# Attention and two feed-forward layers on one core: raw words' places in another order, small softmax operations on DVE, layer 1's weight casts on POOL

## The chip, the cores and the metric

The kernel runs on one core of a Trainium2 chip. A core has the engines PE (matrix products), DVE, ACT and POOL (element-wise work), SP (which issues the DMA transfers here) and DMA queues, all running beside each other and tied by semaphores. The metric is the device time of one execution in microseconds, smaller is better. PE has a clock that the chip grants: 2.4 GHz, or 1.2 GHz at the half level.

## The reference

Attention with 4 batches, 8 heads, 576 positions and 64 values per head; its output, as 2304 tokens of 512 values, goes through two feed-forward layers of width 2048. All inputs are float32.

```python
scores = scale * np.matmul(q, k.transpose(0, 1, 3, 2))
mask_local = (rel >= 0) & (rel < 32)                          # heads 0 to 3
mask_strided = (rel >= 0) & (pos[None, :] % 32 == pos[:, None] % 32)   # heads 4 to 7
scores = np.where(masks[None], scores, -1000000000.0)
attn = np.exp(scores - np.max(scores, axis=-1, keepdims=True))
attn = attn / (np.sum(attn, axis=-1, keepdims=True) + 1e-09)
x = np.matmul(attn, v)             # as (2304, 512)
...
h = np.maximum(x @ w_in, 0.0)      # layer 1
x = h * h @ w_out
...
h = x @ w_in                       # layer 2, weights of its own
P = a[0] + a[1] * h + a[2] * h * h + a[3] * h * h * h
Q = 1.0 + np.abs(b[0]) * np.abs(h) + np.abs(b[1]) * h * h
out = P / (Q + 1e-6) @ w_out
```

## The kernel before

**Precision.** Every operand of layer 1 and layer 2 is kept as a high part (PE's rounded float32 form, `fp32r`) and a low part, the rest. A product is three matmuls: high by high, high by low, low by high.

**Blocks and units.** The tokens are cut into 6 blocks of 384 columns (`j`), the width of 2048 into 16 tiles of 128 (`f`). `h_unit` (matmuls at L457) makes the hidden tile `f` of a block in 12 matmuls, into one PSUM bank `h`; ACT makes its relu `r` (L467) and square, then the high part `gh` (L474), and DVE or POOL the low part `gl` (L475). `o_unit1` (L497) adds the tile's share to four output banks `acc` in 12 matmuls, two steps later. Layer 2 does the same from 523 us of the profile on, with the rational function on DVE.

**Attention.** There are 48 groups of two heads and up to two tiles, 12 for a batch, taken in pairs (a and b). A group is: scores on PE (`ps_s`, L296); their maxima on DVE (L307); these scaled by -1/8 (L308, on POOL); exponentials on ACT with the scaled maximum as bias, which also sum up (L320); 1e-9 added to the sums (L328, on POOL); the reciprocal on DVE (L329); the scaling of the exponentials on POOL (L331); transposes on PE (`ps_t`, L338), a copy (L344, L346); the products with v on PE (`ps_v`, L354); the output's high part on ACT (L379) and low part on DVE (L380). L308, L328 and L329 work on the group's small tile `sm`, up to 4 columns each. The first 12 groups run ahead of layer 1 (`at_slot`), the others are dealt out as pieces between the units of layer 1 (`at_piece`).

**Weights of layer 1.** They lie in DRAM as 64-bit words and come during block 0 as 32 halves of 512 KB (in a name like `wraw_7_1`, 7 is the tile `f`; 0 is its share of w_in, which `h_unit` needs, 1 its share of w_out, for `o_unit1`). `wq` sets their order: 0_0, 1_0, 2_0, 0_1, 3_0, 1_1 and so on; 16 to 27 are 9_0, 7_1, 10_0, 8_1, 11_0, 9_1, 12_0, 10_1, 13_0, 11_1, 14_0, 12_1, and 15_0, 13_1, 14_1, 15_1 are last. `load_raw` (L189) issues the loads on SP in that order; the scheduler may reorder them. The list `homes` names the place in SBUF into which each half's raw words go: a tile that will later hold the high (`h12`) or low part (`l12`) of the weights of a tile `f`, free until then, or, with `None`, one of three stage buffers. A half may only be loaded when its place has been read by whoever had it before.

`to_f32` turns a half into float32: ACT L201 takes the absolute value, scaled; DVE L202, L203 and L204 put the bits together (the intermediate lies in a PSUM bank, `bits`, for layer 1, in SBUF for layer 2). `split_w` then makes the high part `wh` (on ACT at L218 for every fourth half, on POOL at L220 otherwise) and the low part `wl` by subtraction (L221, on POOL but for the first four). From block 1 on, layer 2's weights go through the same functions and out to DRAM.

**Order.** The tile framework's scheduler sets each engine's order from the program's order and its own costs. An engine runs its list strictly in order; an instruction that waits holds all behind it. There are 7 PSUM banks named `ps`; in block 0, `acc` holds four, and `ps_s`, `ps_t`, `ps_v` and `h` share three.

Of the kernel before, what the change touches and what calls it, by code (L numbers as in the profile page):

```python
# [14 lines left out]
ALU = mybir.AluOpType  # L15
# [11 lines left out]
NF = DFF // P  # L27
# [129 lines left out]
def moe_kernel(ctx, tc, qk, vp, w1, w2, a, b, masks, eye, out):  # L157
    nc = tc.nc
# [54 lines left out]
    def split_w(wh, wl, wf):  # L213

        halves[0] += 1
        n = halves[0]
        if n % 4 == 0:
            nc.scalar.copy(wh, wf)  # L218
        else:
            nc.gpsimd.tensor_scalar(wh, wf, 1.0, 0.0, ALU.mult, ALU.add)  # L220
        (nc.vector if n <= 4 else nc.gpsimd).tensor_tensor(wl, wf, wh.bitcast(F32), ALU.subtract)  # L221
# [79 lines left out]
    def at_max(n):  # L301
        g, s = groups[n], st[n]
        nn = s["nn"]
        if n >= LATE:
            nc.vector.tensor_tensor(s["to"], s["to"], s["mask"], ALU.add)
        sm = s["sm"] = apool.tile([P, 16], F32, tag="sm", name=f"sm{g.name}", bufs=6)
        nc.vector.tensor_reduce(sm[: g.nq, 0:nn], s["ps"], AX.X, ALU.max)  # L307
        nc.gpsimd.tensor_scalar(sm[: g.nq, 4 : 4 + nn], sm[: g.nq, 0:nn], -1.0 / 8.0, 0.0, ALU.mult, ALU.add)  # L308

    def at_exp(n):  # L310
        g, s = groups[n], st[n]
# [13 lines left out]
    def at_norm(n):  # L325
        g, s = groups[n], st[n]
        sm, nn = s["sm"], s["nn"]
        nc.gpsimd.tensor_scalar(sm[: g.nq, 8 : 8 + nn], sm[: g.nq, 8 : 8 + nn], 1.0, 1e-9, ALU.mult, ALU.add)  # L328
        nc.vector.reciprocal(sm[: g.nq, 12 : 12 + nn], sm[: g.nq, 8 : 8 + nn])  # L329
        r = sm[: g.nq, 12 : 12 + nn, None].to_broadcast([g.nq, nn, g.nk])  # L330
        nc.gpsimd.tensor_tensor(s["e"], s["e"], r, ALU.mult)  # L331
# [62 lines left out]
    def at_slot(n):  # L394

        load_groups(n + 4)
        if n % 2 == 0:
            at_scores(n)
        at_max(n)
        if n == 2:  # L400
            warm_up(2)
        for m in range(max(0, n - 4), n):
            if n - m == lags(m)[1]:
                at_values(m)
        for m in range(max(0, n - 4), n):
            if n - m == lags(m)[0]:
                at_transpose(m)
        at_exp(n)
        for m in range(max(0, n - 4), n):
            if n - m == lags(m)[1]:  # L410
                at_out(m)
        at_norm(n)
# [14 lines left out]
    def at_piece(piece):  # L427
        nonlocal slot
        if isinstance(piece, int):
            at_scores(piece)  # L430
            for n in (piece, piece + 1):
                at_max(n)
                at_exp(n)
                at_norm(n)
            load_qk(piece // 2 + 2)
            return
        v, t = piece
        if v < NG:
            at_values(v)
            slot = max(slot, v + 5)  # L440
        if t < NG:
            at_transpose(t)
        if v < NG:
            at_out(v)
            if v % 2 and v // 2 + 2 >= AHEAD_PAIRS:
                load_v(v // 2 + 2)
# [81 lines left out]
    def load_co():  # L528
# [9 lines left out]
    homes = [  # L538
        ("h8", 0), ("h9", 0), ("h15", 1), ("h14", 3), ("h13", 5), ("h12", 7), ("h11", 9), ("l11", 9), ("h10", 11), ("l10", 10), ("l9", 11), ("l8", 12),
        ("l15", 13), ("l14", 14), ("l13", 15), ("l12", 16),  # L540
    ]
    homes += [(c + str(f), 0) for f in (12, 13, 14, 15, 14, 15) for c in "hl"] + [(None, 0)] * 4
    raws = []

    def load_raw(done):
# [11 lines left out]
    def feed_w(n):  # L557
        for _ in range(n):
            load_raw(fed[0])
            if fed[0] < len(wq):  # L560
                f, part = wq[fed[0]]
                c = slice(part * DM, (part + 1) * DM)
                wh, wl = wt[0, f] if part else w_place(0, f)
                split_w(wh[:, c], wl[:, c], to_f32(0, f, part, raws[fed[0]]))
                fed[0] += 1
# [14 lines left out]
    def spill_w(f, part):  # L580

        wf = to_f32(1, f, part, load_w(1, f, part))
        parts = [stage.tile([P, DM], F32R, tag="w32", bufs=3, name=f"sp{c}{f}_{part}") for c in "hl"]
        split_w(*parts, wf)
        for z, t in enumerate(parts):
            nc.sync.dma_start(w2_dram[z, f][:, part * DM : (part + 1) * DM], t.bitcast(F32))
# [161 lines left out]
```

## Time and profile before

| what | value |
|---|---|
| median of 3 runs | 929.36 us (928.68 to 929.71) |
| the profiled execution | 929.01 us, of which 927.2 us from the first to the last instruction |
| busy: PE, DVE, POOL, ACT | 899.6, 674.2, 599.1, 548.1 us |
| chain of work that ended last, by engine | DVE 44%, PE 43%, POOL 4%, ACT 4%, DMA 3%, issue 2% |
| its lines | L624 24%, L457 20%, L497 17%, L626 9%, L635 7%, all others 2% or less |

The profile is one execution. The shares are means over stages with different limits, so the time is read by stage: the first 42 us load operands and do the first groups of the attention; from 42 us layer 1's block 0 runs while its weights are converted; from 146 us layer 1's blocks 1 to 5, with the rest of the attention and the conversion of layer 2's weights; from 523 us layer 2.

### The profile page before, as it was taken

The page shows a single profiled execution, that of the slowest core. Times are in us where ns is not written, and L with a number is a line of the kernel's source. Part 1 is how long each engine was busy: PE and PEld are TensorE (multiplying, and loading weights), DVE is VectorE, ACT ScalarE, POOL GpSimd, SP SyncE. Part 2 cuts the span into 40 slices and gives each one's busy share as a digit, 9 for nine tenths or more (in the row PEclk, how much of TensorE's full clock was granted, in tenths as well). Part 3 has the DMA queues.
Part 4 walks back from the last instruction along what each step waited for, and adds up shares of the span by engine and source line. Part 5 has one row for each costly group of instructions (what it writes and reads, how often), then busy time and mean ns, then how long its engine had stood idle before and what let it go on. Part 6 is the DMA issues. An engine that isn't in the chain of part 4 may idle for free.

```text
span 927.2 us, 14645 instructions
## 1 busy us (share of the span) xinstructions
PE 899.6 (97%) x5232; PEld 825.7 (89%) x5232; DVE 674.2 (73%) x792; ACT 548.1 (59%) x1392; POOL 599.1 (65%) x643
## 2 busy tenths in 40 slices
PE   7799889999999999999999999999999999999998
PEld 4698789998998899999999999899999899899896
DVE  3887774645554554635312689999999999999997
ACT  5785564445444444433324577676776777777774
POOL 3676664554554545544333488888888888888885
PEclk9799899999999999999999999999999999999999
DMA  7863235444444543442377620010010100100000
GB/s 282 316 231 121 92 109 177 160 144 155 131 147 140 174 121 122 162 138 78 123 254 253 218 70 9 18 43 10 23 37 10 51 19 1 43 1 1 35 1 34
DMA packets 40104, 98.55 MB, mean 106 GB/s; under 512 B 4704, under 2 KB 11616, under 8 KB 40032
## 3 DMA queue, kind: packets, MB, share of 16 engines
q1 hardware_dynamic: 40032, 97.62, 31.5%
q8 instruction: 41, 0.67, 0.3%
q14 instruction: 31, 0.25, 0.1%
HBM read 71.39 MB, written 26.21 MB: 105 GB/s over the span
## 4 chain that ended last, share of the span: by engine, by line
DVE 44%; PE 43%; POOL 4%; ACT 4%; DMA 3%; issue 2%; POOLq 0%; SPq 0%; DVEq 0%; ACTq 0%
DVE rq L624 24%; PE h L457 20%; PE acc L497 17%; DVE p L626 9%; DVE rq L635 7%; PE ps_s L296 2%; PE ps_v L354 2%; POOL wl L221 2%; PE ps_t L338 2%; ACT e L320 1%; DVE wraw L204 1%; DMA qk<-in_qk 1%; DMA wraw<-in_w 1%; DVE bits L203 1%; ACT w L201 1%
## 5 line engine op out<-in xcount | busy, mean ns | idle before, releaser
L457 PE MATMUL h<-xh,wh 128*128 128x384 f32 x768 | 264.8, 345 | 3.8 <-ACT r L467 2.3
L457 PE MATMUL h<-xh,wl 128*128 128x384 f32 x768 | 259.6, 338 | 0.0
L457 PE MATMUL h<-xl,wh 128*128 128x384 f32 x768 | 259.1, 337 | 0.0
L624 DVE RECIPROCAL rq<-w 128x384 f32<-128x384 f32 x96 | 243.9, 2541 | 17.3 <-POOL w L622 17.3
L457 PEld LDWEIGHTS h<-xh,wh 128*128 128x128 f32 x768 | 145.8, 190 | 12.0 <-issue 2.6
L457 PEld LDWEIGHTS h<-xl,wh 128*128 128x128 f32 x768 | 145.8, 190 | 3.8
L457 PEld LDWEIGHTS h<-xh,wl 128*128 128x128 f32 x768 | 145.4, 189 | 0.0
L643 POOL TENSOR_TENSOR gl<-rq,gh 128x384 fp32r<-128x384 f32 x96 | 114.7, 1195 | 40.1 <-ACT gh L642 40.1
L475 POOL TENSOR_TENSOR gl<-r,gh 128x384 fp32r<-128x384 f32 x75 | 76.1, 1015 | 88.4 <-ACT gh L474 73.1
L497 PE MATMUL acc<-gh,wl 128*128 128x384 f32 x384 | 129.5, 337 | 2.2 <-POOL wl L221 2.2
L497 PE MATMUL acc<-gh,wh 128*128 128x384 f32 x384 | 129.3, 337 | 1.3 <-ACT wh L218 0.9
L497 PE MATMUL acc<-gl,wh 128*128 128x384 f32 x384 | 128.5, 335 | 0.0
L622 POOL TENSOR_TENSOR w<-w,sq 128x384 f32<-128x384 f32 x96 | 97.8, 1019 | 46.7 <-ACT sq L619 46.7
L623 POOL TENSOR_TENSOR p<-p,hs 128x384 f32<-128x384 f32 x96 | 115.0, 1198 | 0.0
L657 PE MATMUL acc<-wh,gl 128*128 128x512 f32 x288 | 114.0, 396 | 0.3 <-POOL gl L643 0.3
L657 PE MATMUL acc<-wl,gh 128*128 128x512 f32 x288 | 113.7, 395 | 0.0
L657 PE MATMUL acc<-wh,gh 128*128 128x512 f32 x288 | 112.1, 389 | 0.5 <-ACT gh L642 0.5
L642 ACT CAST gh<-rq 128x384 fp32r<-128x384 f32 x96 | 49.4, 515 | 106.5 <-DVE rq L635 106.5
L471 DVE TENSOR_TENSOR r<-r 128x384 f32<-128x384 f32 x75 | 51.7, 689 | 81.9 <-ACT r L467 81.5
L626 DVE SCALAR_TENSOR_TENSOR p<-p,co,hs 128x384 f32<-128x384 f32 x96 | 100.0, 1042 | 0.0
L467 ACT ACTIVATE r<-h 128x384 f32<-128x384 f32 x91 | 44.9, 493 | 91.7 <-PE h L457 84.1
L474 ACT CAST gh<-r 128x384 fp32r<-128x384 f32 x91 | 46.9, 515 | 64.9 <-DVE r L471 64.4
(77 smaller groups left out, 1577.7 us busy)
## 6 DMA issues: line engine op xcount, KB each, us to landing
wraw<-in_w SPq DMA_DIRECT2D x64, 512.0 KB, 4.3
w_scratch<-sph SPq DMA_DIRECT2D x32, 256.0 KB, 4.1
w_scratch<-spl SPq DMA_DIRECT2D x32, 256.0 KB, 3.3
wh<-w_scratch SPq DMA_DIRECT2D x16, 512.0 KB, 3.6
wl<-w_scratch SPq DMA_DIRECT2D x16, 512.0 KB, 4.6
v<-in_vp SPq DMA_DIRECT2D x24, 256.0 KB, 4.2
qk<-in_qk SPq DMA_DIRECT2D x12, 416.0 KB, 4.1
x_scratch<-x SPq DMA_DIRECT2D x24, 192.0 KB, 2.5
```

What stands on the lines that cost most here:

```text
L457: nc.tensor.matmul(ps[:, :TB], w[:, c], x[:, kk, :], start=(kk == 0 and i == 0), stop=(kk == KT - 1 and i == 2))
L471: nc.vector.tensor_tensor(h, h, h, ALU.mult)
L475: low = lambda: (nc.vector if psum_h or j == 0 else nc.gpsimd).tensor_tensor(gl, h, gh.bitcast(F32), ALU.subtract)
L497: nc.tensor.matmul(acc[j][e][:, :TB], w[:, c], g, start=(f == 0 and i == 0), stop=(f == NF - 1 and i == 2))
L622: keep(nc.gpsimd.tensor_tensor(w, w, sq, ALU.add))
L623: keep(nc.gpsimd.tensor_tensor(p1, p1, hs, ALU.mult))
L624: keep(nc.vector.reciprocal(rq, w))
L626: keep(nc.vector.scalar_tensor_tensor(p1, p1, a1, hs, ALU.add, ALU.mult))
L635: keep(nc.vector.scalar_tensor_tensor(rq, p1, a0, rq, ALU.add, ALU.mult))
L642: keep(nc.scalar.copy(gh, rq))
L643: keep(nc.gpsimd.tensor_tensor(gl, rq, gh.bitcast(F32), ALU.subtract))
L657: nc.tensor.matmul(p, g[:, t * P : (t + 1) * P], w[:, c], start=(f == 0 and i == 0), stop=(f == NF - 1 and i == 2))
```

## The change

Three edits. (1) The halves 16 to 27 get places in another order, and three of them, with the number 23 to 25, stage buffers instead. (2) The scaling of the maxima (L308) and the addition to the sums (L328) are DVE's instead of POOL's, in all 48 groups. (3) Every fourth cast stays on ACT only for layer 2's weights; the 8 of layer 1's are POOL's. The arithmetic is the same.

```diff
-        if n % 4 == 0:
+        if n % 4 == 0 and n > 2 * NF:
             nc.scalar.copy(wh, wf)
         else:
             nc.gpsimd.tensor_scalar(wh, wf, 1.0, 0.0, ALU.mult, ALU.add)
...
-        nc.gpsimd.tensor_scalar(sm[: g.nq, 4 : 4 + nn], sm[: g.nq, 0:nn], -1.0 / 8.0, 0.0, ALU.mult, ALU.add)
+        nc.vector.tensor_scalar(sm[: g.nq, 4 : 4 + nn], sm[: g.nq, 0:nn], -1.0 / 8.0, 0.0, ALU.mult, ALU.add)
...
-        nc.gpsimd.tensor_scalar(sm[: g.nq, 8 : 8 + nn], sm[: g.nq, 8 : 8 + nn], 1.0, 1e-9, ALU.mult, ALU.add)
+        nc.vector.tensor_scalar(sm[: g.nq, 8 : 8 + nn], sm[: g.nq, 8 : 8 + nn], 1.0, 1e-9, ALU.mult, ALU.add)
...
-    homes += [(c + str(f), 0) for f in (12, 13, 14, 15, 14, 15) for c in "hl"] + [(None, 0)] * 4
+    homes += [(x, 0) for x in ("h12", "h13", "h14", "h15", "l15", "l14", "l13", None, None, None, "h15", "l15")] + [(None, 0)] * 4
```

Three places of the order that the scheduler makes of it. Names: `wraw_7_1` is a half's raw words, `sm_0_0` the small tile of the group with heads 0 and 1 (the first number) and part 0 (the second), `sm_1_0` its partner's. A number at the end tells buffers apart.

SP's list, the loads behind those of 9_0, in block 0. Before:

```order
L189 DMA wraw_12_0_962<-in_w 128x1024
L189 DMA wraw_15_0_1242<-in_w 128x1024
L264 DMA v_2_2_863<-in_vp 128x512
L189 DMA wraw_13_1_1244<-in_w 128x1024
L189 DMA wraw_14_1_1246<-in_w 128x1024
L529 DMA co<-in_a 128x4
L251 DMA qk_0_1_941<-in_qk 128x832
L530 DMA co<-in_b 128x2
L189 DMA wraw_10_1_964<-in_w 128x1024
L189 DMA wraw_9_1_960<-in_w 128x1024
L189 DMA wraw_8_1_956<-in_w 128x1024
L189 DMA wraw_7_1_952<-in_w 128x1024
```

After, from 9_0 on:

```order
L189 DMA wraw_9_0_724<-in_w 128x1024
L189 DMA wraw_7_1_734<-in_w 128x1024
L189 DMA wraw_10_0_800<-in_w 128x1024
L189 DMA wraw_8_1_810<-in_w 128x1024
L189 DMA wraw_10_1_964<-in_w 128x1024
L189 DMA wraw_13_0_1024<-in_w 128x1024
L264 DMA v_2_2_869<-in_vp 128x512
L189 DMA wraw_11_1_1034<-in_w 128x1024
```

7_1 stood last of the twelve rows, behind 10_1, 9_1 and 8_1; it now stands next to 9_0, and 8_1 and 10_1 follow before 13_0.

DVE's list at the first pair of batch 1 (the groups 0_0 and 1_0), between the halves 8_1, 11_0 and 9_1. Before:

```order
L307 TENSOR_REDUCE sm_0_0_1205<-ps_s_0_0_1193 96x4
L202 TENSOR_SCALAR bits_1_1075<-w_0_8_1_1074 128x512
L307 TENSOR_REDUCE sm_1_0_1216<-ps_s_1_0_1194 96x4
L203 SCALAR_TENSOR_TENSOR bits_1_1075<-wraw_8_1_956,bits_1_1075 128x512
L204 SCALAR_TENSOR_TENSOR wraw_8_1_956<-wraw_8_1_956,bits_1_1075 128x512
L329 RECIPROCAL sm_0_0_1205<-sm_0_0_1205 96x4
L202 TENSOR_SCALAR bits_0_1085<-w_0_11_0_1084 128x512
L203 SCALAR_TENSOR_TENSOR bits_0_1085<-wraw_11_0_958,bits_0_1085 128x512
L204 SCALAR_TENSOR_TENSOR wraw_11_0_958<-wraw_11_0_958,bits_0_1085 128x512
L329 RECIPROCAL sm_1_0_1216<-sm_1_0_1216 96x4
```

After:

```order
L307 TENSOR_REDUCE sm_0_0_1213<-ps_s_0_0_1201 96x4
L204 SCALAR_TENSOR_TENSOR wraw_8_1_810<-wraw_8_1_810,bits_1_1079 128x512
L308 TENSOR_SCALAR sm_0_0_1213<-sm_0_0_1213 96x4
L307 TENSOR_REDUCE sm_1_0_1224<-ps_s_1_0_1202 96x4
L202 TENSOR_SCALAR bits_0_1091<-w_0_11_0_1090 128x512
L308 TENSOR_SCALAR sm_1_0_1224<-sm_1_0_1224 96x4
L203 SCALAR_TENSOR_TENSOR bits_0_1091<-wraw_11_0_872,bits_0_1091 128x512
L328 TENSOR_SCALAR sm_0_0_1213<-sm_0_0_1213 96x4
L204 SCALAR_TENSOR_TENSOR wraw_11_0_872<-wraw_11_0_872,bits_0_1091 128x512
L329 RECIPROCAL sm_0_0_1213<-sm_0_0_1213 96x4
L202 TENSOR_SCALAR bits_1_1151<-w_0_9_1_1150 128x512
L328 TENSOR_SCALAR sm_1_0_1224<-sm_1_0_1224 96x4
```

L308 and L328 of both groups now stand in DVE's list, each with a step of a half's conversion ahead of it.

PE's list at tile 8's accumulation, where the values of one group (`ps_v_2_2`) and the transposes of its partner (`ps_t_3_2`) lie. Before:

```order
L354 MATMUL ps_v_2_2_1291<-at_2_2_1131,v_2_2_863 64x72 x2
L497 MATMUL acc_0_0_763<-gh_0_8_1178,wh_8_874 128x384
L497 MATMUL acc_0_0_763<-gl_0_8_1179,wh_8_874 128x384
L497 MATMUL acc_0_1_764<-gh_0_8_1178,wh_8_874 128x384
L497 MATMUL acc_0_1_764<-gl_0_8_1179,wh_8_874 128x384
L497 MATMUL acc_0_0_763<-gh_0_8_1178,wl_8_875 128x384
L338 MATMUL ps_t_3_2_1294<-ident,e_3_2_935 72x72 x2
L497 MATMUL acc_0_1_764<-gh_0_8_1178,wl_8_875 128x384
L497 MATMUL acc_0_2_765<-gh_0_8_1178,wh_8_874 128x384
L497 MATMUL acc_0_2_765<-gl_0_8_1179,wh_8_874 128x384
L497 MATMUL acc_0_2_765<-gh_0_8_1178,wl_8_875 128x384
L457 MATMUL h_0_10_1322<-xh_0_220,wh_10_1032 128x384
```

After:

```order
L354 MATMUL ps_v_2_2_1291<-at_2_2_1137,v_2_2_869 64x72 x2
L338 MATMUL ps_t_3_2_1294<-ident,e_3_2_945 72x72 x2
L497 MATMUL acc_0_0_765<-gh_0_8_1186,wh_8_884 128x384
L497 MATMUL acc_0_0_765<-gl_0_8_1187,wh_8_884 128x384
L497 MATMUL acc_0_0_765<-gh_0_8_1186,wl_8_885 128x384
L497 MATMUL acc_0_1_766<-gh_0_8_1186,wh_8_884 128x384
L457 MATMUL h_0_10_1322<-xh_0_220,wh_10_1036 128x384
```

The transposes now follow the values at once, where five matmuls of `acc` stood between; four instead of nine of `acc` are left before `h` of tile 10, the rest comes behind it.

## Rows read from the trace of the kernel before

**Rows 1.** Stages: start:end, us, busy PE, PEld, DVE, ACT, POOL (instructions), PEclk, DMA, GB/s

```profile
0.00:42.00 42.00, 31.20 (x248) 20.53 (x249) 24.74 (x65) 27.93 (x131) 19.88 (x47) 0.86 0.87 305
42.00:75.00 33.00, 33.00 (x223) 30.59 (x222) 28.43 (x55) 25.62 (x74) 23.53 (x32) 0.97 0.58 196
75.00:146.00 71.00, 61.68 (x378) 56.31 (x377) 51.07 (x89) 41.09 (x119) 44.49 (x52) 0.93 0.36 118
146.00:523.00 377.00, 374.85 (x2398) 359.02 (x2397) 177.71 (x303) 166.79 (x477) 182.45 (x217) 1.00 0.47 156
523.00:927.00 404.00, 398.82 (x1993) 359.24 (x1991) 392.21 (x284) 286.67 (x593) 328.71 (x298) 1.00 0.09 30
```

**Rows 2.** Timeline of PE: start, us, instruction, [idle before <-releaser]

```profile
80.88 0.41 PE L457 MATMUL h<-xh,wh 128*128 128x384 f32 x1 [0.40 <-ACT r L467]
...
88.67 0.66 PE L457 MATMUL h<-xh,wh 128*128 128x384 f32 x1 [1.89 <-ACT r L467]
...
96.35 0.35 PE L354 MATMUL ps_v<-at,v 72*64 72x72 f32 x4 [1.76 <-ACT e L320]
...
97.58 0.44 PE L497 MATMUL acc<-gh,wh 128*128 128x384 f32 x1 [0.88 <-ACT wh L218]
...
99.28 0.69 PE L497 MATMUL acc<-gh,wl 128*128 128x384 f32 x1 [0.74 <-POOL wl L221]
...
117.78 0.55 PE L354 MATMUL ps_v<-at,v 128*64 128x96 f32 x8 [0.88 <-ACT e L320]
...
118.79 0.44 PE L497 MATMUL acc<-gh,wh 128*128 128x384 f32 x1 [0.46 <-POOL wh L220]
...
121.05 0.44 PE L497 MATMUL acc<-gh,wl 128*128 128x384 f32 x1 [1.47 <-POOL wl L221]
...
141.89 0.55 PE L338 MATMUL ps_t<-ident,e 96*128 96x96 f32 x4 [0.83 <-ACT e L320]
```

**Rows 3.** Stages in which PE's clock is at half; columns as in rows 1

```profile
88.60:92.00 3.40, 3.33 (x10) 3.36 (x11) 3.26 (x6) 1.64 (x3) 1.98 (x2) 0.50 0.18 70
98.80:105.60 6.80, 6.32 (x21) 6.20 (x22) 4.06 (x10) 1.86 (x8) 5.87 (x7) 0.50 0.25 80
```

**Rows 4.** Timeline of ACT at the late half

```profile
85.83 2.31 ACT L201 ACTIVATE w<-wraw 128x512 f32<-128x512 f32 x4 [2.91 <-DMA wraw<-in_w]
88.05 0.47 ACT L467 ACTIVATE r<-h 128x384 f32<-128x384 f32 x1
```

**Rows 5.** Lines, 42 to 146 us: shapes xcount | busy, mean ns | idle before <-releasers

```profile
L221 POOL TENSOR_TENSOR wl<-wraw,wh 128x512 fp32r<-128x512 f32 x28 | 38.2, 1364 | 8.0 <-ACT wh L218 6.5
L220 POOL TENSOR_SCALAR wh<-wraw 128x512 fp32r<-128x512 f32 x21 | 14.7, 702 | 16.5 <-DVE wraw L204 16.1
L331 POOL TENSOR_TENSOR e<-e,sm 96x512 f32<-96x512 f32 (+2 forms) x12 | 11.6, 971 | 2.1 <-DVE sm L329 1.7 <-PE ps_v L354 0.4
...
L218 ACT CAST wh<-wraw 128x512 fp32r<-128x512 f32 x8 | 5.4, 671 | 5.1 <-DVE wraw L204 5.1
...
L202 DVE TENSOR_SCALAR bits<-w 128x512 int32<-128x512 int32 x28 | 19.2, 685 | 4.8 <-ACT w L201 4.4
...
L329 DVE RECIPROCAL sm<-sm 96x4 f32<-96x4 f32 (+2 forms) x11 | 1.9, 172 | 11.9 <-POOL sm L328 11.9
```

**Rows 6.** Waits, 42 to 146 us: engine, line <- releaser: us, times, longest

```profile
ACT e L320 <- POOL sm L308: 9.5, 5, 4.0
...
POOL sm L328 <- ACT e L320: 6.8, 6, 2.0
```

**Rows 7.** L202 in layer 2's words: ns min/median/max; then one beside POOL (timeline)

```profile
L202 DVE TENSOR_SCALAR w<-w x32: 510/774/1019, 144.2 to 444.6; 128x512 int32<-128x512 int32 x32
...
165.95 1.00 POOL L475 TENSOR_TENSOR gl<-r,gh 128x384 fp32r<-128x384 f32 x1
...
166.25 0.99 DVE L202 TENSOR_SCALAR w<-w 128x512 int32<-128x512 int32 x1 [1.16 <-ACT w L201]
```

**Rows 8.** Waits of DVE, 8 to 42 us; columns as in rows 6

```profile
DVE sm L329 <- POOL sm L328: 5.3, 6, 1.4
```

## The prediction

> **What bounds the kernel now.** I read the stages first. In [rows 1] the last 404 us are DVE's: it is busy 392.21 of them, with layer 2's rational function, which the change does not touch. The stage before, 146 to 523 us, is PE's: 374.85 of 377 us busy, at full clock. So the end moves only by what PE does earlier, before 146 us. From 75 to 146 us PE is busy only 61.68 of 71 us, and its clock column says 0.93. From 42 to 75 us PE is busy all the time, and the first 42 us are the loading of the first operands and the first softmax groups. So the change must win or lose in two places: the front, and 75 to 146 us, where PE is idle for 71 - 61.68 = 9.3 us.
>
> Second, PE's own timeline there, for the idle time ahead of single matmuls, [rows 2]. Nine gaps make up 9.31 us, and they fall into five places: 80.88 and 88.67 us (0.40 + 1.89, a free PSUM bank that waits for ACT's relu, L467); 96.35, 97.58 and 99.28 us (1.76 + 0.88 + 0.74, the first softmax group pair of batch 1, then the weights of the accumulation); 117.78, 118.79 and 121.05 us (0.88 + 0.46 + 1.47, the second pair, the same two causes); 141.89 us (0.83, the third pair's exponentials).
>
> Third, the clock. [Rows 3] are the two stretches in which PE is granted half of it, 1.2 instead of 2.4 GHz: 3.40 us that begin with the matmul after the 1.89 us gap, and 6.80 us that begin inside the gaps at 96 to 99 us. PE is busy 3.33 and 6.32 us there at half speed, so full speed would have saved 1.7 and 3.2 us. The three gaps at 117 to 121 us are followed by no such stretch. Idle time and half clock together are 9.3 + 4.9 = 14.2 us: the most that can be had after 75 us.
>
> **Raw words' places.** In block 0, layer 1's weights come as raw words, 32 halves one after the other, and each half goes ACT (L201), DVE (L202 to L204), POOL or ACT (the cast), POOL (the subtraction L221). Before, the half 7_1 is issued last of four on SP, behind 10_1, 9_1 and 8_1, since the place it gets frees late; after, it stands behind 9_0 and takes a place with no wait. [Rows 4] show what the late load does: ACT sits idle for 2.91 us at L201, with the DMA as the releaser, then runs four L201 in a row for 2.31 us, and only then, at 88.05 us, the relu (L467) for which PE waits until 88.67 us. Without it the gap of 1.89 us goes, and with it the stretch at half clock that follows it at once, 1.7 us. Term A: -1.9 - 1.5 = -3.4 us (of the 1.7 I leave 0.2, as half a matmul more or less may stay). What is late next: halves 15_0, 12_1 and 15_1 now wait for places that the halves before them leave, and in the new order ACT's L201 of 15_0 stands ahead of the exponentials of the second pair, so a late half could again hold ACT there. I cost that within term D and with rival 4.
>
> **Casts of layer 1 on POOL.** Eight casts go from ACT to POOL: [rows 5] give 671 ns each on ACT and 702 ns on POOL, so 5.4 us off ACT and 5.6 us onto POOL, of 104 us from 42 to 146 us. ACT's queue is what holds the relu at 80.88 us, a cast long: term B, -0.4 us. POOL is busy 44.49 of the 71 us from 75 to 146 us ([rows 1]), 63%, and gives off 21 small operations in exchange. The cover is POOL's slack; if it goes, the accumulation at 97.58 and 118.79 us waits longer for L220, by up to one cast, 0.70 us, each.
>
> **Small operations on DVE.** 96 of them move: per group the scaling of the maxima (L308) and the addition to the sums (L328). 21 of them fall between 42 and 146 us, 27 in the front, the rest after 146 us, where DVE is busy 177.71 of 377 us until 523 us and PE has work: nothing, with plus or minus 1 us for the three softmax waits that PE still has there.
>
> What it removes, 42 to 146 us: DVE idles 11.9 us ahead of the reciprocal L329, as POOL's L328 ended last, and ACT's exponentials idle 9.5 us as POOL's L308 ended last, once for 4.0 us ([rows 5, 6]): the small operation stands behind a subtraction of 1.36 us on POOL. Not all of the 11.9 us is POOL's. In the softmax the reciprocal needs the exponentials anyway, and L328's own wait for them is 6.8 us ([rows 6]). So DVE gets back between 11.9 - 6.8 = 5.1 and 11.9 us; I take the middle, 8.5 us. To this comes the wait at L202 that the late half caused, 4.4 us ([rows 5]), in all 12.9 us.
>
> What it adds: 21 operations on DVE. No row shows a 4-column tensor_scalar on DVE. The nearest is the reciprocal of the same tile, 172 ns, so 21 x 0.17 = 3.6 us. The open price is whether such an operation can start beside a running POOL instruction. [Rows 7] show that a DVE tensor_scalar between SBUF tiles can be held: L202 of layer 2's words takes 510 to 1019 ns, median 774, and the one shown, begun at 166.25 us, ends at 167.24 us, 0.29 us after the subtraction on POOL that had begun at 165.95 us; the same L202 with its result in PSUM takes 685 ns in layer 1's words ([rows 5]). The bounds of a hold are nothing and what is left of POOL's instruction. POOL's long ones there are 28 of 1.364, 21 of 0.702 (and the 8 casts added) and 12 of 0.971 us; weighted by length, what is left on average is (28 x 1.86 + 29 x 0.49 + 12 x 0.94) / (2 x 70.1) = 0.55 us, and POOL is busy about two thirds of the time (23.53 + 44.49 of 104 us, [rows 1]): 0.37 us each, 7.8 us for 21. So DVE gives back 12.9 and is charged 3.6 to 11.4 us: a relief of 9.3 to 1.5 us. I take the middle of the hold, as the row that shows it has 512 columns and the added ones 4. In no case of these is DVE fuller than before; the point at which the change turns on itself is a mean hold of (12.9 - 3.6) / 21 = 0.44 us.
>
> The Trainium skill bears on this open price ("SBUF — State Buffer", section "Who interferes with whom"): DVE and GpSimd share one pair of ports as an exclusive lock, and tensor_scalar is of the kinds that take it. [Rows 7] agree for 512 columns; no row shows 4 columns. By it the hold would be the full 7.8 us where I take half; if PE gets half of that back, the gain below would be 2 us smaller.
>
> What of this reaches PE: the exponentials start earlier by what POOL's subtraction held L308, and the values (L354) of an earlier group wait for the PSUM bank that these exponentials free. For the second pair, 117 to 121 us, the new order on DVE puts L308 behind one cast step instead of behind a subtraction on POOL, so the exponentials can come some 1 us earlier; the gap of 0.88 us goes, and those of 0.46 and 1.47 us, in which a cast and a subtraction stand behind L328 and L331 on POOL, shrink with them. Of 2.8 us I leave 0.8 for ACT's L201 that now stand ahead of the exponentials: term D, -2.0 us. At 141.89 us I leave 0.3 of 0.83: term E, -0.5 us. For the first pair, 96 to 99 us, I expect nothing (term C, 0): its exponentials also come earlier, but on PE the transposes (`ps_t_3_2`) now stand directly behind the values (`ps_v_2_2`), where before five matmuls of an accumulation filled in, and wait at once for the bank that the pair's second exponentials free. So the 3.4 us of gaps and the 3.2 us at half clock stay. The bound of C is -6.6 us, if both go.
>
> **The front.** 27 operations are added on DVE there, 27 x 0.17 = 4.6 us, against 5.3 us of waits for L328 that go in part ([rows 8]). POOL is busy 19.88 of 42 us there ([rows 1]), so holds are rarer; but the chain maximum, exponential, sum, reciprocal sets PE's start directly, and a hold of 0.5 us would stand in it. Term F: +1.0 us, from -1 (two hops between engines less for each group) to +3.
>
> **Sum.** -3.4 - 0.4 + 0 - 2.0 - 0.5 + 1.0 = -5.3 us. The profiled execution took 929.01 us, 0.35 below the median of 929.36; against the median the sum gives 924.06, so 924.0 us.
>
> **Rivals.** 1, the forecast: 920 to 927.5 us. 2, the first pair gains too: if its exponentials come early enough, gap and half clock go, and nearly all of the 14.2 us is had, less some front: 929.4 - 14.2 + 1 = 916 us. For it: both half-clock stretches begin with idle time, and C is only as firm as the order on PE. Against: five matmuls fewer to fill in. 3, slower: DVE becomes what PE waits for, because each small operation is held by POOL. It needs a mean hold above 0.44 us; at 0.55 us, the mean rest of a POOL instruction each time, DVE is 21 x (0.55 - 0.44) = 2.3 us behind in the feed after 42 us, so that A's and D's gains go into later halves; in the front the same hold for the share that POOL is busy, 27 x 0.55 x 0.47 = 7.0 us, and 4.6 us of its own stand against 5.3 us of waits, 6.3 us more, of which the part on the softmax chain, about half, reaches PE; B and E, 0.9 us, stay: 929.4 + 2.3 + 3 - 0.9 = 933.8, some 933 us. For it: [rows 7]. Against: 4 columns, and L308 comes while POOL often waits. The lock of the page named above would be this mechanism, at its worst. 4, the places do nothing: the feed takes one half in some 3.4 us whichever place is free, so the wait for 7_1 only turns up at 15_0 or 12_1, behind ACT's L201, and the other gains pay for the front: 929 us. 5, what is won before 146 us is lost again, as something else than PE sets the start of layer 2: also 929 us. Against it: 374.85 of 377 us.
>
> **How the numbers follow.** Chances: forecast 0.44, rival 2 0.21, rival 3 0.18, rival 4 0.11, rival 5 0.06. The predicted time is that of the first, 924.0 us. The range reaches to rival 2's 916 below, and above to 931, through rivals 4 and 5 and half of rival 3's cases; it leaves out some 0.2. A measurement of this kernel tells about 0.2%, 1.9 us, from no change. Faster than 927.5: the first two, 0.65, nearly all of both, 0.64. Within 0.2%: rivals 4 and 5 and the edge of the first, 0.17. Slower than 931.2: rival 3 and a bit more, 0.19.
>
> **What would show it.** A: no idle ACT ahead of L201 at about 85 us, no matmul with a gap over 1 us near 88 us, no half clock behind it. B: no wait for the relu of about 0.4 us. C: idle PE of 3 us around the first pair, and half clock behind it; if both are gone, rival 2. D, E: gaps at the second and third pair under 1 us. Holds: durations of the added L308 and L328 on DVE beside POOL's instructions, near 0.17 us if there is none, 0.5 us and more if there is. F: the time of the first matmul of layer 1, some 1 us later. The prediction is wrong if PE's idle time from 75 to 146 us has not fallen below 7 us, or if the stage 146 to 523 us is no longer 375 us of PE's work.

## The result and the profile after

The changed kernel takes 917.67 us (median of 4 runs, 917.29 to 918.42) against 929.02 us (928.45 to 929.71) for the kernel before: a ratio of 0.9879, 95% interval 0.9861 to 0.9896, or 11.35 us less. The forecast was 924.0 us, 5.4 us less than the 929.36 us it was reckoned from. The time lies in the range, and the direction was right, but the gain is over twice the forecast: rival 2's outcome, not the one that was predicted.

The profiled execution took 917.56 us with a span of 915.8 us, against 927.2 us: 11.4 us less. The stages of the kernel after, with the columns of [rows 1] (start:end, us, busy time of PE, PEld, DVE, ACT and POOL, PE's clock, DMA share, GB/s); their limits are set 11 us earlier from the third on, so that the last two are as long as before:

```profile
0.00:42.00 42.00, 29.86 (x242) 19.78 (x244) 27.35 (x88) 27.73 (x127) 13.51 (x19) 0.80 0.83 294
42.00:75.00 33.00, 32.41 (x218) 29.47 (x215) 30.84 (x66) 24.26 (x74) 24.32 (x25) 0.94 0.63 208
75.00:135.00 60.00, 56.78 (x379) 51.95 (x378) 53.74 (x102) 37.89 (x113) 46.10 (x46) 1.00 0.42 141
135.00:512.00 377.00, 376.07 (x2407) 360.70 (x2406) 193.01 (x352) 167.37 (x480) 172.54 (x169) 1.00 0.47 156
512.00:916.00 404.00, 399.11 (x1996) 359.76 (x1994) 391.86 (x284) 287.06 (x594) 328.92 (x299) 1.00 0.09 30
```

The last two stages have the same length by that choice, and PE's work in them is the same within 1.3 us. The gain lies in the third: 60 us where there were 71, PE idle for 60 - 56.78 = 3.2 us instead of 9.3, and the clock at 1.00 all through instead of 0.93. In the first two PE does a little less than before, at a lower clock (0.80 and 0.94 against 0.86 and 0.97).

PE's gaps from 75 us on, where [rows 2] had nine (timeline of PE after):

```profile
94.39 0.32 PE L338 MATMUL ps_t<-ident,e 72*72 72x72 f32 x2 [1.46 <-ACT e L320]
...
110.64 0.55 PE L354 MATMUL ps_v<-at,v 128*64 128x96 f32 x8 [0.74 <-ACT e L320]
...
112.18 0.55 PE L338 MATMUL ps_t<-ident,e 96*128 96x96 f32 x4 [0.62 <-ACT e L320]
...
132.96 0.55 PE L338 MATMUL ps_t<-ident,e 96*128 96x96 f32 x4 [0.41 <-ACT e L320]
```

Four are left, 3.23 us together, all of them waits of the softmax's matmuls for exponentials. The waits for the relu (0.40 and 1.89 us) and all waits of the accumulation for a cast or a subtraction (0.88, 0.74, 0.46, 1.47 us) are gone.

DVE's waits and the two operations that it took over, 42 to 135 us (waits: us, times, longest; lines: shapes, count, busy us, mean ns, idle before):

```profile
DVE sm L328 <- ACT e L320: 2.6, 2, 1.6
...
DVE bits L202 <- ACT w L201: 1.2, 1, 1.2
...
L308 DVE TENSOR_SCALAR sm<-sm 96x4 f32<-96x4 f32 (+2 forms) x11 | 5.3, 490 | 0.0
...
L328 DVE TENSOR_SCALAR sm<-sm 96x4 f32<-96x4 f32 (+2 forms) x11 | 2.9, 262 | 2.7 <-ACT e L320 2.6
```

The wait of L329 for POOL's L328 (11.9 us in [rows 5]) is replaced by 2.6 us in which L328 waits for the exponentials; that at L202 fell from 4.4 to 1.2 us. L308 takes 490 ns on average and L328 262 ns, so some of them are held.

The following table shows when PE began the first matmul of the hidden tile `f` of block 0 (and of block 1, tile 3), read from the traces of single profiled executions. It is used by the experiments too; "places" is the run with the new places alone, "7_1 back" the whole change with 7_1's old place.

| first matmul of | before | after | places | small operations | casts | 7_1 back | without L328 |
|---|---|---|---|---|---|---|---|
| block 0, tile 0 | 42.2 | 43.1 | 41.9 | 44.4 | 41.1 | 44.3 | 42.6 |
| tile 7 | 75.3 | 77.4 | 76.4 | 79.1 | 74.6 | 78.6 | 76.5 |
| tile 9 | 88.7 | 88.2 | 87.8 | 91.3 | 88.2 | 92.2 | 87.3 |
| tile 10 | 101.4 | 95.3 | 94.8 | 103.4 | 100.2 | 102.9 | 94.8 |
| tile 13 | 122.4 | 113.1 | 113.8 | 122.1 | 118.9 | 121.3 | 111.7 |
| block 1, tile 3 | 151.6 | 142.7 | 143.6 | 152.1 | 150.0 | 154.5 | 140.9 |
| block 5, tile 15 | 518.8 | 508.3 | 510.9 | 517.9 | 516.9 | 520.2 | 506.0 |

Between tile 9 and tile 10 the kernel after gains 5.6 us, the largest step, at the place for which the forecast had put 0.

### The profile page after: what moved, and what is told of

Same layout as the page of the kernel before. It is cut to its first block, busy times and chain, and to the rows that moved or that the text cites. A ratio compares the mean times of both kernels' runs of the same rounds, so it can differ in the third digit from the quotient of the medians.

```text
span 915.8 us, 14708 instructions
## 1 busy us (share of the span) xinstructions
PE 894.2 (98%) x5232; PEld 821.7 (90%) x5232; DVE 696.8 (76%) x888; ACT 544.3 (59%) x1384; POOL 585.4 (64%) x555
## 4 chain that ended last, share of the span: by engine, by line
PE 46%; DVE 45%; ACT 4%; DMA 2%; POOL 1%; issue 1%; SPq 0%; ACTq 0%; DVEq 0%; POOLq 0%
DVE rq L624 24%; PE h L457 21%; PE acc L497 18%; DVE p L626 9%; DVE rq L635 7%; PE ps_t L338 2%; PE ps_v L354 2%; PE ps_s L296 2%; ACT e L320 2%; DVE wraw L204 1%; DVE bits L203 1%; DMA co<-in_b 1%; DMA x_scratch<-x 1%; DMA qk<-in_qk 1%; PE acc L657 1%
## 5 line engine op out<-in xcount | busy, mean ns | idle before, releaser
L475 POOL TENSOR_TENSOR gl<-r,gh 128x384 fp32r<-128x384 f32 x75 | 77.7, 1038 | 80.4 <-ACT gh L474 74.4
L471 DVE TENSOR_TENSOR r<-r 128x384 f32<-128x384 f32 x75 | 56.9, 759 | 80.9 <-ACT r L467 80.6
```

Source lines behind the costliest of these rows:

```text
L471: nc.vector.tensor_tensor(h, h, h, ALU.mult)
L475: low = lambda: (nc.vector if psum_h or j == 0 else nc.gpsimd).tensor_tensor(gl, h, gh.bitcast(F32), ALU.subtract)
```

## The experiments

**Which part does it.** Theory L: the half 7_1, late, made not only the gap of 1.89 us but a backlog in the conversion of weights, and the gaps and the half clock at the first softmax pair of batch 1 came from that. Theory S: those come from POOL standing in the softmax's way, and the small operations on DVE remove them. The kernels take the three edits of the change one by one, and places with casts.

Places alone:

```diff
-    homes += [(c + str(f), 0) for f in (12, 13, 14, 15, 14, 15) for c in "hl"] + [(None, 0)] * 4
+    homes += [(x, 0) for x in ("h12", "h13", "h14", "h15", "l15", "l14", "l13", None, None, None, "h15", "l15")] + [(None, 0)] * 4
```

> The places alone. Theory L (the late half): the gaps and the half clock at the first softmax pair of batch 1 were the late half's backlog on DVE, so the places alone win term A and nearly all of the first pair: 7 to 9 us less than before (about 921), no half clock from 75 us on, PE idle from 75 to 146 us about 4 to 5 us. Theory S (the softmax's way over POOL): the first pair's gaps come from POOL standing between maxima and exponentials, so the places alone win only term A, 3 to 4 us (about 925.5), with a stretch of half clock left behind the first pair.

Small operations alone:

```diff
-        nc.gpsimd.tensor_scalar(sm[: g.nq, 4 : 4 + nn], ...
+        nc.vector.tensor_scalar(sm[: g.nq, 4 : 4 + nn], ...
...
-        nc.gpsimd.tensor_scalar(sm[: g.nq, 8 : 8 + nn], ...
+        nc.vector.tensor_scalar(sm[: g.nq, 8 : 8 + nn], ...
```

> The two small operations on DVE alone. Theory L: 1 to 3 us less than before (about 927), as the gap of 1.9 us near 88 us, the half clock behind it and most of the first pair's gaps stay, and the front loses 1 to 2 us. Theory S: 4 to 6 us less (about 924), with the first pair's gaps down by 2 us and no half clock behind them.

Casts alone:

```diff
-        if n % 4 == 0:
+        if n % 4 == 0 and n > 2 * NF:
```

> The eight casts on POOL alone. Both theories: within 1 us of before (928.5), B's gap of 0.4 us gone, the late half's gap unchanged. If ACT's queue was what made the first pair's exponentials late, 2 us or more.

Places and casts together:

> Places and casts, small operations on POOL as before. Theory L: 8 to 10 us less than before (about 920), within 2 us of the whole change, and the front (first matmul of layer 1, 42.2 us before, 43.1 us after) back at 42.2. Theory S: 4 to 5 us less (about 925).

Places and small operations together, the casts as before:

> Places and small operations, casts as before. The parts add up (theory L with the casts worth nothing): 929 - 8.3 - 3.3 = 917.4 us, the whole change's time within 1.5 us. Rival (the casts take from ACT what the softmax on DVE needs, so the two belong together): 919 to 921 us.

| kernel | median, us (range, runs) | ratio to before (95%) |
|---|---|---|
| places | 920.49 (918.64 to 921.0, 4) | 0.9903 (0.9885 to 0.9921) |
| small operations | 925.57 (923.46 to 927.35, 10) | 0.9962 (0.9951 to 0.9973) |
| casts | 929.53 (926.11 to 931.35, 10) | 1.0004 (0.9992 to 1.0017) |
| places and casts | 921.38 (919.35 to 921.76, 4) | 0.9912 (0.9894 to 0.993) |
| places and small operations | 917.96 (916.77 to 921.42, 4) | 0.9885 (0.9857 to 0.9913) |

The medians of before beside them were 928.82 us (the first four) and 928.84 us. The places win 8.3 us alone, the small operations 3.3 us, the casts nothing, and the first two add up: 917.96 us where 917.4 was expected. Theory L holds: the places alone come out as it said, and the small operations are nearer to its 1 to 3 us than to the 4 to 6 us of theory S. Windows of the run with the places alone, then with the small operations alone, then with the casts alone (columns as in [rows 1]), and at the end PE's two gaps at the first pair with the places alone, and one at the same pair with places and casts (timeline of PE):

```profile
75.00:146.00 71.00, 66.16 (x437) 60.67 (x437) 54.90 (x97) 42.47 (x124) 48.03 (x55) 1.00 0.45 145
...
75.00:110.00 35.00, 30.45 (x179) 28.14 (x178) 28.30 (x54) 19.85 (x56) 22.97 (x23) 0.90 0.37 114
...
75.00:110.00 35.00, 28.37 (x164) 25.56 (x162) 25.23 (x47) 18.64 (x52) 22.68 (x26) 0.90 0.33 115
...
92.53 0.35 PE L354 MATMUL ps_v<-at,v 72*64 72x72 f32 x4 [0.32 <-ACT e L320]
...
93.91 0.32 PE L338 MATMUL ps_t<-ident,e 72*72 72x72 f32 x2 [1.04 <-ACT e L320]
...
95.86 0.43 PE L457 MATMUL h<-xh,wh 128*128 128x384 f32 x1 [2.32 <-POOL e L331]
```

With the places alone PE is idle for 71 - 66.16 = 4.8 us from 75 us on, and its clock is full; with either of the others alone the half clock stays (0.90 of 35 us, so 3.5 us lost). At the first pair the places alone leave 0.32 + 1.04 us of the 3.4 us of gaps, both for exponentials. Two things came out otherwise than expected. With the casts alone the gap of the late half did not stay as it was, it grew from 1.89 to 2.74 us. And with places and casts, though layer 1 begins at 42.3 us as expected, the first pair again has gaps, of 0.99 and 2.32 us, the second one for POOL's scaling (L331), and 3.4 us at half clock behind them: the early half alone does not clear that place when POOL has both the casts and the small operations. In the medians this is 0.9 us, and the runs of the two kernels overlap.

**Is it one half?** The whole change, with the place of 7_1 alone put back, so that it waits for the place of 6_1 again and stands last of its row on SP:

```diff
-    homes += [(x, 0) for x in ("h12", "h13", "h14", "h15", "l15", "l14", "l13", None, None, None, "h15", "l15")] + [(None, 0)] * 4
+    homes += [(x, 0) for x in ("h12", "l12", "h14", "h15", "l15", "l14", "l13", None, None, None, "h15", "l15")] + [(None, 0)] * 4
```

> The whole change, with one place put back: 7_1 gets the place it had (l12), so that its load again stands last of its row on SP; all other halves keep their new places. Theory L (this one late half makes the backlog, the gaps at the first pair and the half clock): 924 to 926.5 us, 6 to 9 us above the whole change, with an idle ACT ahead of L201, DVE idle 3 us or more at L202, PE idle 8 us or more from 75 to 146 us and half clock there. Rival (the other places, 8_1 to 10_1 earlier, make half of it): 920.5 to 922 us.

It took 928.08 us (926.06 to 929.92, 10 runs; before beside it 929.29), ratio 0.9985 (0.9972 to 0.9997). One place takes back 10.4 of the 11.35 us, more than theory L expected: with the late half even the small operations' gain is gone. Its stage from 75 us on, ACT's timeline, and PE's waits from 75 to 146 us (us, times, longest):

```profile
75.00:146.00 71.00, 62.41 (x380) 56.65 (x379) 57.29 (x103) 37.58 (x114) 45.46 (x46) 0.93 0.40 126
...
89.40 2.31 ACT L201 ACTIVATE w<-wraw 128x512 f32<-128x512 f32 x4 [4.54 <-DMA wraw<-in_w]
91.61 0.48 ACT L467 ACTIVATE r<-h 128x384 f32<-128x384 f32 x1
...
PE h L457 <- ACT r L467: 2.8, 1, 2.8
PE acc L497 <- POOL wh L220: 2.2, 2, 1.6
PE ps_t L338 <- ACT e L320: 2.1, 2, 1.3
```

Most of what [rows 1, 2, 4] showed is back: ACT idle, here for 4.54 us, ahead of four L201 in a row, the relu behind them, the wait of 2.8 us for it, waits of the accumulation for a cast, 8.6 us of idle PE and the clock at 0.93. The early places of the other halves do not prevent it: in this kernel 8_1 and 10_1 stand as early as in the changed one. But the first pair is not as it was before. Ahead of its accumulation there are 0.70 and 0.44 us of gaps, and none for its exponentials; the half clock now lies from 91.2 us, at the 2.77 us gap, to 98.1 us, and from 122.0 to 125.4 us, behind the second pair's gaps of 1.55 and 1.29 us:

```profile
91.20:98.10 6.90, 5.87 (x18) 5.90 (x19) 6.66 (x10) 3.60 (x8) 3.96 (x4) 0.51 0.10 38
...
122.00:125.40 3.40, 3.40 (x13) 3.40 (x12) 3.26 (x7) 1.61 (x4) 3.08 (x3) 0.51 0.54 161
```

So this run shows what the one late half costs in all. Of the 12.3 us between the two profiles, 1.2 us are there at layer 1's first matmul already (44.3 against 43.1 us), before the late half can act.

**The front.** The whole change, with POOL keeping both small operations for the first 12 groups:

```diff
-        nc.vector.tensor_scalar(sm[: g.nq, 4 : 4 + nn], ...
+        (nc.vector if n >= FIRST else nc.gpsimd).tensor_scalar(sm[: g.nq, 4 : 4 + nn], ...
...
-        nc.vector.tensor_scalar(sm[: g.nq, 8 : 8 + nn], ...
+        (nc.vector if n >= FIRST else nc.gpsimd).tensor_scalar(sm[: g.nq, 8 : 8 + nn], ...
```

> The whole change, but the first 12 groups keep both small operations on POOL. If the front's loss (term F, first matmul of layer 1 some 1 to 2 us later, and 2.2 to 3.7 us in the run with the small operations alone) is made by the small operations that DVE holds for POOL: 1.5 to 2.5 us below the whole change, 915.5 us. If the front differs from run to run for other reasons: within 0.7 us of the whole change, 917.7 us.

917.47 us (916.52 to 918.94, 4 runs), ratio 0.9872 (0.9855 to 0.9889): the time of the whole change. Its first matmul of layer 1 came at 43.0 us, as in the whole change. Tile 7 began at 77.4 us in both. So the small operations that DVE does there are not what makes the front's loss, as far as four runs can tell.

**Which of the small operations.** Places and casts, with one of the two moved:

```diff
-        nc.gpsimd.tensor_scalar(sm[: g.nq, 4 : 4 + nn], ...
+        nc.vector.tensor_scalar(sm[: g.nq, 4 : 4 + nn], ...
```

> Places, casts and only the scaling of the maxima (L308) on DVE. If the gain that the small operations add lies ahead of the exponentials (they no longer wait for POOL's subtraction): 918 to 919 us, nearly the whole change. If it lies behind them (sums, reciprocal, scaling): 921 us, as with places and casts.

```diff
-        nc.gpsimd.tensor_scalar(sm[: g.nq, 8 : 8 + nn], ...
+        nc.vector.tensor_scalar(sm[: g.nq, 8 : 8 + nn], ...
```

> Places, casts and only the addition to the sums (L328) on DVE. If the gain lies ahead of the exponentials: 920 to 921.5 us, as with places and casts. If behind them, because POOL comes to L331 sooner: 918 to 919 us, and no wait of a hidden tile's matmuls for POOL's L331 (3.1 us in the run with places and casts).

With the maxima alone: 921.21 us (917.62 to 923.34, 4 runs), ratio 0.9907 (0.9879 to 0.9934); with the sums alone: 923.22 us (921.47 to 926.09, 5 runs), ratio 0.9943 (0.9921 to 0.9965). The first expectation did not come true, the second kernel is slower than either, and the comparison decides little: the runs of one kernel lie up to 5.7 us apart, and the slower a run of the first, the lower its mean granted clock (917.62 us at 0.994, 923.34 us at 0.983; this does not say which comes first). Both profiled executions have a stretch at half clock that the whole change has not, or has shorter. A window of the first, then of the second (columns as in [rows 1]):

```profile
110.00:122.00 12.00, 9.35 (x46) 8.85 (x45) 9.85 (x19) 7.21 (x26) 9.35 (x12) 0.72 0.43 149
...
40.00:51.00 11.00, 8.46 (x49) 7.16 (x50) 8.28 (x18) 6.11 (x25) 6.89 (x9) 0.53 0.71 259
```

What they show is that the two operations together are worth some 3 us beside the places (by the medians 2.5 us without the casts, where the runs of the two kernels overlap, and 3.7 us with them, where they do not), and that either alone is not reliably worth anything. The second kernel has no wait of PE for POOL's L331 left from 75 to 146 us, as was expected of it, and is slower all the same. Which of the two matters stays open.

**The hold.** The two operations as scalar_tensor_tensor, of which no hold had been noticed:

```diff
-        nc.vector.tensor_scalar(sm[: g.nq, 4 : 4 + nn], sm[: g.nq, 0:nn], -1.0 / 8.0, 0.0, ALU.mult, ALU.add)
+        nc.vector.scalar_tensor_tensor(sm[: g.nq, 4 : 4 + nn], sm[: g.nq, 0:nn], -1.125, sm[: g.nq, 0:nn], ALU.mult, ALU.add)
...
-        nc.vector.tensor_scalar(sm[: g.nq, 8 : 8 + nn], sm[: g.nq, 8 : 8 + nn], 1.0, 1e-9, ALU.mult, ALU.add)
+        nc.vector.scalar_tensor_tensor(sm[: g.nq, 8 : 8 + nn], sm[: g.nq, 8 : 8 + nn], 1e-9, sm[: g.nq, 8 : 8 + nn], ALU.mult, ALU.add)
```

> The whole change with both small operations written as scalar_tensor_tensor (-1.125 times x plus x; 1e-9 times x plus x), a form that no row shows held for POOL, where the same tile's tensor_scalar was held 5.3 us (L308) and 2.3 us (L328) in all. If the form sets the hold: no L308 or L328 above 0.3 us beside POOL, and 0.5 to 2 us below the whole change, about 916.5. If any DVE operation on that tile is held: durations of 0.6 to 1 us as before, 917.7 us.

(The 5.3 and 2.3 us of this expectation are not holds; 5.3 us is the whole busy time of the 11 L308 in the changed kernel. By 490 and 262 ns on average against 160 ns without a hold, the holds are 3.6 us for L308 and 1.1 us for L328.)

918.39 us (916.17 to 920.0, 4 runs), ratio 0.988 (0.986 to 0.99): no gain. L308 and L328 in that kernel, all 48 of each (ns, least, median, most), and the same L308 in the changed kernel:

```profile
L308 DVE SCALAR_TENSOR_TENSOR sm<-sm x48: 122/151/962, 9.4 to 371.2; 96x4 f32<-96x4 f32 x24, 126x4 f32<-126x4 f32 x16, 72x2 f32<-72x2 f32 x8
...
L328 DVE SCALAR_TENSOR_TENSOR sm<-sm x48: 146/159/1226, 11.6 to 374.3; 96x4 f32<-96x4 f32 x24, 126x4 f32<-126x4 f32 x16, 72x2 f32<-72x2 f32 x8
...
L308 DVE TENSOR_SCALAR sm<-sm x48: 130/159/992, 8.1 to 369.8; 96x4 f32<-96x4 f32 x24, 126x4 f32<-126x4 f32 x16, 72x2 f32<-72x2 f32 x8
```

The form does not set the hold: 962 and 1226 ns at most, as tensor_scalar's 992 ns. The trace of before had shown it already, in L203 of layer 2's words, which stays in SBUF (the same view of the kernel before):

```profile
L203 DVE SCALAR_TENSOR_TENSOR w<-wraw,w x32: 677/692/1387, 145.2 to 445.4; 128x512 int32<-128x512 int32 x32
```

Two of those 32 took 1.38 and 1.39 us, the others 0.68 to 0.69 us; both had begun 0.35 to 0.36 us after a POOL subtraction (L475) had.

**Without L328.** The reciprocal reads the sums directly, once with the casts as in the change and once as before it:

```diff
-        nc.vector.scalar_tensor_tensor(sm[: g.nq, 8 : 8 + nn], sm[: g.nq, 8 : 8 + nn], 1e-9, sm[: g.nq, 8 : 8 + nn], ALU.mult, ALU.add)
```

> As the run before it, with the addition of 1e-9 left out (the sums are 1 or more, so that float32 does not change by it), the reciprocal reading the sums directly. 48 operations of 0.16 us less on DVE, of which 10 or 11 lie from 42 to 140 us: 0 to 1.5 us below the run with both as scalar_tensor_tensor, about 916.

With the casts as before:

```diff
-        if n % 4 == 0 and n > 2 * NF:
+        if n % 4 == 0:
```

> The same, with layer 1's casts as before, every fourth on ACT. If the casts are worth nothing either way: within 0.7 us of the run with them, 916 us. If ACT's relief counts once POOL is out of the small operations: 1 to 2 us above it.

913.01 us (912.19 to 915.55, 4 runs), ratio 0.9821 (0.9805 to 0.9837), and 914.95 us (913.32 to 915.78, 4 runs), ratio 0.9843 (0.9826 to 0.9859). Both beat the changed kernel, by more than was expected: the first is 5.4 us below the run with both operations as scalar_tensor_tensor. The second is 1.9 us above the first, as it would be if ACT's relief counted, but the runs of the two overlap. In the profiles (918.92 us with L328, 915.55 us without) 1.7 of the 3.3 us by which the spans differ are won ahead of layer 1's first matmul (44.3 and 42.6 us), nearly all the rest by block 1, tile 3 (144.1 and 140.9 us). The stretch from 40 to 47 us of the changed kernel, of the run with scalar_tensor_tensor, of the one without L328 and with the casts on POOL, and of the kernel before with the casts alone; then 0 to 47 us of the second and the third (columns as in [rows 1]):

```profile
40.00:47.00 7.00, 5.31 (x32) 4.84 (x32) 6.71 (x16) 5.18 (x22) 2.55 (x4) 0.58 0.86 313
...
40.00:47.00 7.00, 5.04 (x29) 4.49 (x26) 7.00 (x17) 5.38 (x22) 3.07 (x4) 0.51 0.98 353
...
40.00:47.00 7.00, 6.09 (x54) 5.05 (x53) 6.98 (x17) 6.88 (x27) 3.76 (x5) 1.00 0.89 341
...
40.00:47.00 7.00, 6.74 (x52) 5.83 (x52) 6.29 (x15) 6.19 (x21) 4.53 (x8) 1.00 0.82 299
...
0.00:47.00 47.00, 35.54 (x259) 24.33 (x260) 31.17 (x97) 30.52 (x138) 15.21 (x21) 0.78 0.83 291
...
0.00:47.00 47.00, 38.38 (x280) 26.27 (x281) 31.62 (x87) 32.25 (x143) 16.57 (x23) 0.82 0.83 295
```

In the first two PE has about half its clock from 40 to 47 us, in the third all of it: 32, 29 and 54 matmuls in the same 7 us. But the half clock is not gone in the third, it lies earlier: over 0 to 47 us the two clocks are 0.78 and 0.82, which is 47 x 0.04 = 1.9 us. And the fourth has the full clock from 40 to 47 us with L328 in place. So that the shorter chain of the first groups keeps the clock up is not shown, and how the 5.4 us come about stays open; that the eight runs without L328 lie between 912.2 and 915.8 us, and the four of the changed kernel between 917.3 and 918.4 us, is measured.

## Why the prediction was wrong

**What bounds it: right.** The end moved mostly by what PE won before 146 us, and the stages behind kept their length within 2.5 us. Nearly the whole gain is in the stretch that the forecast named.

**A and B (-3.8 us): right.** The gaps of 0.40 and 1.89 us and the 1.7 us at half clock are gone, 4.0 us. The run with 7_1 put back has the long gap again, of 2.77 us, with half clock behind it. The gap of 0.40 us is also gone with the casts alone; a gain of 0.4 us cannot be told from nothing in that run's time.

**C (0): the step that failed.** It said that the first pair's 3.4 us of gaps and 3.2 us of half clock stay, since on PE the transposes now follow the values at once. One gap of 1.46 us is left of the 3.4, and no half clock: 5.1 us, of the 6.6 that stood as its bound. The gap that is left is the one that the step described, ahead of the transposes (`ps_t`). The step looked for the cause of all three gaps at the place, in the order on PE, though the prediction itself had read two of them from [rows 2] as waits for the weights of the accumulation: those of 0.88 and 0.74 us wait for a cast and a subtraction of the half 8_1. DVE had sat idle for 3.25 us ahead of 7_1's L202, and what stood behind it in its list ran late: the last conversion step (L204) of 8_1 ended at 95.0 us before and at 90.6 us after. First the two rows of the kernel before, then the one after (timelines of DVE):

```profile
86.53 0.69 DVE L202 TENSOR_SCALAR bits<-w 128x512 int32<-128x512 int32 x1 [3.25 <-ACT w L201]
...
94.34 0.69 DVE L204 SCALAR_TENSOR_TENSOR wraw<-wraw,bits 128x512 int32<-128x512 int32 x1
...
89.89 0.67 DVE L204 SCALAR_TENSOR_TENSOR wraw<-wraw,bits 128x512 int32<-128x512 int32 x1
```

The maxima of the first group (L307) stand in the same list, at 91.84 us before and 89.29 us after, so the exponentials of the third gap, of 1.76 us, were late too: with the places alone, POOL still doing L308, it is down to 0.32 us. The price of the late half was counted once, where ACT waited, and not at the halves queued behind it. Had it been, term A would have carried some -8 us, as the run with the places alone shows (-8.3 us); 7_1 put back costs 10.4 us.

**D and E (-2.5 us): about right in size.** D measured -1.45 us (2.81 to 0.74 + 0.62 us), E -0.4 us (0.83 to 0.41 us). No part alone gives D: at the second pair the places alone leave 1.42 + 0.83 us, the small operations alone 2.09 us. The late half that was feared there came, as ACT sat idle for 4.19 us ahead of 15_0's L201 (timeline of ACT after):

```profile
108.53 0.67 ACT L201 ACTIVATE w<-wraw 128x512 f32<-128x512 f32 x1 [4.19 <-DVE sm L308]
```

It cost the exponentials little, since the L308 that they wait for ended at 108.45 us: only this one L201 stands between.

**F (+1.0 us): size within its bounds, reason not shown.** Tile 7 begins 2.1 us later in the profile after. But the run with the places alone is 1.1 us late there too, and with POOL keeping the small operations in the front the time and tile 7 stay the same. The first matmul of layer 1 came at 41.1 to 42.3 us in the four profiles in which POOL does all the small operations, and at 41.8 to 44.4 us in the five in which DVE does all of them, one execution each. The clock differs as well, but it does not put the kernels in order: here from 40 to 47 us the kernel before and the places alone, to set beside the first row of the last experiment (columns as in [rows 1]).

```profile
40.00:47.00 7.00, 6.37 (x42) 5.61 (x41) 6.96 (x15) 5.69 (x21) 3.93 (x7) 0.70 0.72 268
...
40.00:47.00 7.00, 6.50 (x33) 5.62 (x34) 6.03 (x12) 4.39 (x16) 4.23 (x7) 0.51 0.76 297
```

PE gets 0.70 of its clock in the first and 0.51 in the second, 2.1 and 3.4 us lost, and 0.58 in the kernel after, 2.9 us lost; yet the places alone reach tile 7 ahead of the kernel after. What makes the front late stays open.

**After 146 us (plus or minus 1 us): low.** From block 1, tile 3 (8.9 us ahead) to block 5, tile 15 (10.5 us ahead) the kernel after wins another 1.6 us. The places alone win nothing there (8.0 and 7.9 us ahead), the small operations alone 1.4 us; the forecast had put this at nothing, within 1 us, for the waits for exponentials. PE's waits for them there fell from 2.1 to 0.8 us.

Together: -4.0 - 5.1 - 1.45 - 0.4 + 2.1 - 1.6 = -10.45 us of the 11.4 us by which the spans differ; the last 0.9 us comes after block 5, in layer 2, which the change does not touch; with the casts alone, which won nothing, the profile has 1.0 us there too.

**The open price: the middle was right.** The hold was put at half of 0.37 us for each added operation. Measured from 42 to 135 us, 11 of each: (490 + 262) / 2 - 160 = 0.22 us, with 160 ns as an operation without a hold takes. It is well below the 0.44 us at which DVE would have lost, so rival 3 did not come about. **The casts** were worth nothing that could be measured, alone (1.0004), beside the places (920.49 and 921.38 us) or in the whole change (917.96 without, 917.67 us with them); without L328 the 1.9 us between the two kernels leave it open. **Rival 2** had the right time, 916 us, and nearly the right reason: gap and clock at the first pair go; but by the early places alone, with the small operations still on POOL.

## What to carry to other kernels

A late transfer in a strict queue is priced through everything behind it: follow its delay to each later consumer, here two gaps ten microseconds on and the clock behind them, before costing those gaps by what is seen beside them. When a forecast says that a stall stays, the releaser of each single gap should be checked against it; a gap that waits for another engine's late work is not kept by the order on the waiting engine. And before a small operation is moved to another engine, ask whether it is needed: leaving L328 out won 5.4 us against the same kernel with it.

## What the runs showed of the hardware

DVE's short operations can be held by POOL's two-operand instructions, and then end just behind them. In the changed kernel, the L308 that began at 91.75 us, 0.36 us into POOL's subtraction, and beside it a reciprocal of the same kind of tile that began in the middle of a POOL multiplication (timelines of DVE and POOL: start, us, instruction):

```profile
91.75 0.98 DVE L308 TENSOR_SCALAR sm<-sm 96x4 f32<-96x4 f32 x1
...
91.39 1.32 POOL L221 TENSOR_TENSOR wl<-wraw,wh 128x512 fp32r<-128x512 f32 x1
...
58.93 0.17 DVE L329 RECIPROCAL sm<-sm 126x4 f32<-126x4 f32 x1
...
58.27 1.03 POOL L331 TENSOR_TENSOR e<-e,sm 126x504 f32<-126x504 f32 x1
```

The first ends at 92.73 us, 0.02 us after POOL's at 92.71 us; 12 of the 96 added operations show this, with 0.36 to 1.22 us instead of 0.16, all behind a tensor_tensor on POOL. The Trainium skill ("SBUF — State Buffer", section "Who interferes with whom") has this as an exclusive lock on ports that DVE and GpSimd share; the trace agrees, for 4 columns too, and for scalar_tensor_tensor as for tensor_scalar. The reciprocal was not held: 0.17 us, begun and ended within POOL's 1.03 us, and so in all five cases that the trace has. Whether POOL's own tensor_scalar holds DVE no row decides.

Runs of one kernel can lie far apart, and PE's mean granted clock goes with it: with the maxima alone on DVE four runs took 917.62, 920.39, 922.04 and 923.34 us at mean clocks of 0.994, 0.989, 0.987 and 0.983. Half clock followed the gaps of 1.89 us in the kernel before and of 2.77 us in the run with 7_1 put back; after one of 2.09 us in the run with the small operations alone, and after one of 2.74 us in the run with the casts alone, ahead of the same hidden tile 9, the clock stayed full (timeline of PE, then the window behind the gap, columns as in [rows 1], for either run):

```profile
119.61 0.55 PE L354 MATMUL ps_v<-at,v 128*64 128x96 f32 x8 [2.09 <-ACT e L320]
...
119.00:128.00 9.00, 8.05 (x58) 7.38 (x59) 8.19 (x16) 7.45 (x25) 6.77 (x7) 1.00 0.10 31
...
88.16 0.41 PE L457 MATMUL h<-xh,wh 128*128 128x384 f32 x1 [2.74 <-ACT r L467]
...
88.00:96.00 8.00, 4.60 (x28) 4.31 (x28) 6.34 (x10) 3.98 (x16) 4.40 (x7) 1.00 0.00 0
```

So the length of the gap alone does not decide it. What does was not tried.
